# Seven small edits to a mixer kernel at once: load order and row work at the beginning, two ops moved between engines, p0 of even rows at the tails, slab differences spread over the first unit, one VectorE op ahead of the deferred work

## Chip, cores, metric

The kernel runs on one core of one Trainium2 chip. The metric is device time in microseconds (us), the median of several executions. Before the change it is 502.78 us (502.75 to 502.86, four executions). The granted clock of TensorE is recorded with each execution.

## The reference

With `xn` the layer norm of `x` (2048 rows of 576, bf16), the kernel computes a spectral mixer and a gated MLP of the same rows and combines them:

```python
xn = layernorm(x)
s  = irfft2(rfft2(xn) * (w_r + 1j * w_i))            # "A"
z  = gelu(xn @ w_in)                                  # 576 -> 4608
z1, z2 = z[..., :2304], layernorm(z[..., 2304:])
g  = (w_sp @ z2) + b_sp[:, None]                      # 2048 x 2048, over the rows
out = x + s * silu((z1 * g) @ w_out)
```

## The kernel before

TensorE (PE) runs one long list of matmuls.

**The beginning.** Loads are issued from two queues, SyncE (SP) and ScalarE (ACT). Rows are normalized on VectorE (DVE) in blocks of 128, `m` = 0..15; POOL (GpSimd) computes `(var + eps) ** -0.5`.

```python
nc.scalar.dma_start(out=ident[:], in_=cd_id.ap())
for m0, m1 in ((0, 1), (1, 2), (2, 4)):                       # x rows 0, 1, 2-3
    nc.sync.dma_start(out=XC[0][:, m0:m1, :], in_=xv[:, m0:m1, :])
for n in range(2):                                            # first two column groups of w_in, two loads each
    load_win_main(WIN2[...], slice(...), nc.scalar)
for g in range(3):
    (load_win if g else load_win_tail)(WIN2[...], slice(...)) # first the tails of the same groups
    if g == 0:
        nc.sync.dma_start(out=CDSD, in_=cd_cdsd.ap()...)      # the DFT matrix that p0 needs
    load_x(g + 1)
```

A DMA completion semaphore is used again eight loads later, so the cdsd load cannot be issued before x rows 2-3 have landed.

**The row pairs.** PE alternates between "chunks" of the MLP (`fill`: four full matmuls of 384 columns and a half-height "tail") and the first DFT of the rows (`p0`). p0 needs the transposed row (PE transpose, evicted from PSUM by ScalarE) and its fold, sum and difference of two halves, on VectorE:

```python
for m in range(2, MT):
    if m % 2 == 0:
        xpose(m + 1)
    p0_fold(m)                       # DVE, two tensor_tensor
    if m + 3 < MT:
        ln1(m + 3)                   # DVE: two bn_stats, one bn_aggr; POOL: var + eps, pow
    if m + 2 < MT:
        ln1_apply(m + 2)             # DVE: (x - mean) * rstd
    if m % 2 == 0:
        fill(1, 0)
        p0(m, True)
        fill(1, 0, lambda: p0_pair(m))   # tails of four chunks, then of p0(m) and p0(m+1)
    else:
        p0(m, False); p0_out(m)
        fill(1, 0)
        if m + 1 < MT:
            xpose(m + 1)
        fill(1, 0)
```

Chunks and transposes share four PSUM buffers, given out in the order in which they come free.

**The units.** The product over rows (`w_sp @ z2`) runs as 27 units, nine for each of three column blocks (units 0, 9, 18 begin a block; the third block has 256 columns instead of 384). Each unit has seven products P1, P6, P5, P7, P2, P4, P3 of eight matmuls, on sums and differences of the inputs. `tsum` makes such differences of the z2 blocks (which=2 on POOL), `slab_sums` those of `w_sp`. The order on VectorE is the program's order:

```python
def tsum(u, which):                       # cut
    if which == 0:   nc.vector.tensor_tensor(out=t, in0=zblk(p, 1, 1), in1=zblk(p, 0, 1), op=ALU.subtract)
    elif which == 1: nc.vector.tensor_tensor(out=t, in0=t2, in1=zblk(p, 0, 0), op=ALU.subtract)
    else:            nc.gpsimd.tensor_tensor(out=t, in0=zblk(p, 1, 0), in1=t2, op=ALU.subtract)

def main(u):                              # cut
    prod(a, "P1", zblk(p, 0, 0))          # PE
    nc.scalar.activation(out=p1, in_=a, func=ACT.Identity)
    nc.gpsimd.tensor_tensor(out=p1b, in0=p1, in1=B[1], op=ALU.add)
    prod(b, "P6", tb[u, 0])
    add(p1a, b, p1)                       # DVE, reads PSUM
    nc.gpsimd.tensor_tensor(out=ux, in0=p1a, in1=B[0], op=ALU.add)
    while later:                          # deferred DVE work of the stage before
        later.pop()()
    tsum(u + 1, 0)                        # DVE
    prod(c, "P5", zblk(p, 0, 1))
    prod(b, "P7", tb[u, 1], True)
    add(p1, b, p1b)                       # DVE; b is then free for P4
    u_sum(1, 1, c, p1)
    prod(a, "P2", zblk(p, 1, 0), True)
    tsum(u + 1, 2)                        # POOL
    u_sum(0, 0, a, B[0])                  # DVE
    prod(b, "P4", tb[u, 2], True)
    ...
    prod(c, "P3", zblk(p, 1, 1), True)    # reads the slabs that slab_sums(i, 0, 2) makes
```

Before unit 0: `tsum(0, 0)`, `tsum(0, 2)`, `tsum(0, 1)`, `slab_sums(0, 0, 2)`, `slab_sums(1, 0, 2)`; `slab_sums(2, 0, 2)` is in `later`.

## Time and profile before

| what | before |
|---|---|
| time, median | 502.78 us |
| span of the profiled execution | 501.5 us |
| PE busy | 492.1 us, 98% |
| row pair (start of p0 to start of p0 two rows on) | 5.20 us |
| PE waits from 206 to 216 us | 0.77 + 0.50 us |

From the page of the kernel before: the span, PE's busy time, and the granted TensorE clock in 40 slices (9 is 90% or more).

```profile
span 501.5 us, 9327 instructions
...
PE 492.1 (98%) x3454; PEld 310.4 (62%) x3454; DVE 329.8 (66%) x714; ACT 171.0 (34%) x355; POOL 210.8 (42%) x281
...
PEclk9999999999999999999999999999999999999999
...
PE 89%; ACT 4%; DVE 3%; DMA 2%; issue 1%; SPq 0%; DVEq 0%; ACTq 0%
```

PE is the limit: only time in which PE waits can be won. Where I give such waits, they are the gap between the starts of two matmuls, less the columns of the first at 2.4 per ns, the rate of this trace's back-to-back matmuls (384 columns every 0.162 us). A half-height matmul is counted with half its columns, since these start in pairs (at 10.58 and 10.58, 10.70 and 10.71 us in the trace of e11). The profiler's own idle times, in brackets in the lines below, are somewhat shorter, since it models the ends of matmuls.

From the timeline of the beginning (columns: start in us, duration, engine, line, operation, output and input, shape, count; in brackets the idle time of the engine just before and what ended it):

```profile
7.01 0.35 SPq L243 DMA_DIRECT2D AR<-c_cdsd  x1
7.02 0.82 DVE L258 BATCH_NORM_STATS2 st_165<-AR 128x6 f32<-128x288 bf16 x2 [0.66 <-DMA AR<-in_A_x_dram]
...
8.40 1.07 POOL L251 TENSOR_TENSOR rs<-ve,mhalf 128x1 f32<-128x1 f32 x2
...
8.99 0.41 DVE L281 TENSOR_SCALAR AR<-AR,mv_151,rs 128x512 bf16<-128x512 bf16 x1 [0.91 <-POOL rs L251]
...
10.32 0.66 PE L317 MATMUL pa<-AR 128*128 128x290 bf16 x4 [0.41 <-DMA AR<-c_cdsd]
...
12.05 0.32 PE L441 MATMUL ph<-AR 64*128 64x384 bf16 x1 [0.36 <-ACT AR L293]
```

x rows 2-3 land at 7.0 us; only then is cdsd issued, and the first p0 (L317) waits for it until 10.32. Row 1's pow (the first of the two at 8.40) stands behind row 2's variance op, and a chunk (L441) waits at 12.05 for a PSUM buffer, that is for ScalarE's eviction of a transpose (L293).

From the timeline of PE alone, one row pair:

```profile
19.56 0.81 PE L441 MATMUL ph<-AR 128*128 128x384 bf16 x4
20.47 0.67 PE L317 MATMUL pa<-AR 128*128 128x290 bf16 x4
20.98 1.24 PE L441 MATMUL ph<-AR 128*128 128x384 bf16 x8
...
22.40 0.67 PE L317 MATMUL pa<-AR 128*128 128x290 bf16 x4
...
25.66 0.67 PE L317 MATMUL pa<-AR 128*128 128x290 bf16 x4
```

Four matmuls of 384 columns take 0.65 us, but the p0 after the chunk at 19.56 starts 0.91 us after it: 0.26 us of waiting, in each of six row pairs (20.47 to 25.66: 5.19 us).

From the timeline around unit 0, and around the start of unit 18:

```profile
206.73 2.62 POOL L588 TENSOR_TENSOR AR<-Z_74,AR 128x1024 bf16<-128x1024 bf16 x1 [2.47 <-DVE AR L584]
207.28 3.21 DVE L523 TENSOR_TENSOR AR<-AR 128x1024 bf16<-128x1024 bf16 x2
...
211.02 1.46 PE L600 MATMUL pm<-AR 128*128 128x384 bf16 x8 [0.60 <-DVE AR L604]
...
427.17 0.81 DVE L667 TENSOR_TENSOR AR<-AR 128x576 bf16<-128x576 bf16 x1
...
427.90 0.68 DVE L584 TENSOR_TENSOR AR<-Z_74 128x1024 bf16<-128x1024 bf16 x1
...
428.87 2.13 POOL L588 TENSOR_TENSOR AR<-Z_74,AR 128x1024 bf16<-128x1024 bf16 x1
```

The slab differences (L523) take 0.68 us each elsewhere; two of them take 3.21 us beside POOL's subtraction (L588), and a product then waits.

### The profile page before, as it was taken

What the parts mean: (1) busy time and instruction counts of PE and PEld (TensorE: products, weight loads), DVE (VectorE), ACT (ScalarE), POOL (GpSimd) and SP (SyncE); (2) the same over time, 40 slices, a digit from 0 to 9 for tenths busy, and PEclk for the clock granted to TensorE, in tenths of its full rate; (3) what the DMA queues carried; (4) which work ended last, traced back from release to release, by engine and by line L of the source; (5) the groups of instructions that cost most, each with busy time, mean ns of one, the idle gap of its engine ahead of it and who ended that gap; (6) DMA issues with size and microseconds to landing.
All of it is one profiled execution on the core that took longest, in us unless ns stands there. A gap on an engine that the chain in (4) does not pass through costs nothing.

```text
span 501.5 us, 9327 instructions
## 1 busy us (share of the span) xinstructions
PE 492.1 (98%) x3454; PEld 310.4 (62%) x3454; DVE 329.8 (66%) x714; ACT 171.0 (34%) x355; POOL 210.8 (42%) x281
## 2 busy tenths in 40 slices
PE   7999999999999999999999999999999999999996
PEld 2655454555546544456666677666666678888885
DVE  5776588798646473966666547865656637877734
ACT  4878777686868755300000011000000011000001
POOL 2664323434242774554544501445355301666600
PEclk9999999999999999999999999999999999999999
DMA  7961688988373997581112499121121853111202
GB/s 233 322 198 49 241 272 258 320 240 222 121 257 118 212 252 208 182 274 58 38 33 64 110 167 216 39 63 33 35 61 33 171 137 93 48 48 46 80 26 71
DMA packets 86766, 70.82 MB, mean 141 GB/s; under 512 B 39776, under 2 KB 79328, under 8 KB 86464
## 3 DMA queue, kind: packets, MB, share of 16 engines
q1 hardware_dynamic: 80480, 55.69, 41.7%
q0 software_dynamic: 5008, 13.71, 8.2%
q10 hardware_dynamic: 1232, 0.82, 0.5%
q8 instruction: 27, 0.44, 0.4%
q14 instruction: 19, 0.16, 0.1%
HBM read 40.55 MB, written 21.26 MB: 123 GB/s over the span
## 4 chain that ended last, share of the span: by engine, by line
PE 89%; ACT 4%; DVE 3%; DMA 2%; issue 1%; SPq 0%; DVEq 0%; ACTq 0%
PE pm L600 42%; PE po L654 13%; PE ph L537 13%; PE ph L441 12%; ACT AR L322 2%; PE pa L415 2%; PE pb L374 2%; PE pa L317 2%; DMA AR<-in_A_x_dram 1%; PE pa L389 1%; ACT Z_74 L460 1%; DVE AR L523 1%; PE pa L362 1%; ACT AR L293 1%; DMA AR<-c_cdsd 1%
## 5 line engine op out<-in xcount | busy, mean ns | idle before, releaser
L600 PE MATMUL pm<-AR,Z_74 128*128 128x384 bf16 (+1 forms) x864 | 138.7, 308 | 0.0
L604 DVE TENSOR_TENSOR AR<-pm,AR 128x384 f32<-128x384 f32 (+3 forms) x162 | 82.4, 513 | 69.7 <-PE pm L600 66.5
L600 PEld LDWEIGHTS <-Z_74 128*128 128x128 bf16 x864 | 84.5, 98 | 40.6
L600 PE MATMUL pm<-AR 128*128 128x384 bf16 (+1 forms) x648 | 107.0, 308 | 1.0 <-DVE AR L604 0.9
L441 PE MATMUL ph<-AR 128*128 128x384 bf16 (+1 forms) x480 | 89.7, 327 | 1.4 <-ACT AR L293 0.9
L537 PE MATMUL ph<-AR 128*128 128x512 bf16 (+1 forms) x360 | 85.3, 379 | 0.0
L600 PEld LDWEIGHTS <-AR 128*128 128x128 bf16 x648 | 63.4, 98 | 31.9 <-issue 1.7
L614 ACT ACTIVATE AR<-pm 128x384 f32<-128x384 f32 (+1 forms) x27 | 12.3, 454 | 186.7 <-PE pm L600 186.7
L654 PE MATMUL po<-AR 128*128 128x288 bf16 x540 | 66.6, 286 | 0.0
L654 PEld LDWEIGHTS <-AR 128*128 128x128 bf16 x594 | 56.9, 98 | 13.9
L588 POOL TENSOR_TENSOR AR<-Z_74,AR 128x1024 bf16<-128x1024 bf16 x27 | 57.9, 2144 | 13.9 <-PE pm L600 10.6
L441 PEld LDWEIGHTS <-AR 128*128 128x128 bf16 (+1 forms) x480 | 40.1, 97 | 36.2 <-issue 13.2
L557 POOL DMA_DIRECT2D Z1d<-AR x55 | 31.9, 580 | 57.4 <-ACT AR L546 56.6
L615 POOL TENSOR_TENSOR AR<-AR 128x384 f32<-128x384 f32 (+1 forms) x27 | 22.8, 844 | 76.6 <-ACT AR L614 75.1
L537 PEld LDWEIGHTS <-AR 128*128 128x128 bf16 (+1 forms) x360 | 30.5, 97 | 29.3 <-issue 6.3
L546 ACT ACTIVATE AR<-ph 128x512 bf16<-128x512 f32 x72 | 42.1, 594 | 17.7 <-PE ph L537 16.8
L460 ACT ACTIVATE Z_74<-ph 128x384 bf16<-128x384 f32 x66 | 32.0, 502 | 23.8 <-PE ph L441 23.5
L657 ACT ACTIVATE TH<-po 128x576 f32<-128x576 f32 x15 | 9.8, 650 | 77.8 <-PE po L654 77.8
L618 POOL TENSOR_TENSOR AR<-AR 128x384 f32<-128x384 f32 (+1 forms) x27 | 30.4, 1128 | 11.9 <-DVE AR L604 11.9
L611 DVE TENSOR_TENSOR AR<-AR 128x384 bf16<-128x384 bf16 (+1 forms) x108 | 31.7, 335 | 0.9
L663 DVE SCALAR_TENSOR_TENSOR AR<-TH,po 128x576 bf16<-128x576 f32 x15 | 11.3, 754 | 30.0 <-ACT TH L657 29.9
L669 POOL DMA_DIRECT2D out_dram<-AR x12 | 6.6, 548 | 52.5 <-DVE AR L667 46.0
(183 smaller groups left out, 494.5 us busy)
## 6 DMA issues: line engine op xcount, KB each, us to landing
Z1d<-AR POOLq DMA_DIRECT2D x55, 128.0 KB, 3.9
AR<-Z1d SPq DMA_DIRECT2D x36, 192.0 KB, 3.1
AR<-in_A_x_dram SPq DMA_DIRECT2D x18, 144.0 KB, 3.1
AR<-in_B_w_out_dram SPq DMA_DIRECT2D x1, 2592.0 KB, 10.0
Ad<-AR POOLq DMA_DIRECT2D x16, 144.5 KB, 3.8
AR<-Ad SPq DMA_DIRECT2D x4, 578.0 KB, 6.0
AR<-in_A_w_r_dram SPq DMA_DIRECT2D x16, 144.5 KB, 4.2
AR<-in_A_w_i_dram SPq DMA_DIRECT2D x16, 144.5 KB, 3.9
```

The costliest lines, as they stand in the source:

```text
L441: nc.tensor.matmul(self.ph[:], lhsT=xnT[rows, self.m, ks, :], rhs=WIN2[rows, ks, n * ZC:(n + 1) * ZC], start=start, stop=stop)
L460: nc.scalar.activation(out=zc, in_=ph[:], func=ACT.Gelu_apprx_tanh)
L537: nc.tensor.matmul(self.ph[:].rearrange("p (a t) -> p a t", a=4), lhsT=wb[rows, ks, (fi % WG) * P:(fi % WG + 1) * P], rhs=xnT[rows, 4 * tq ...
L546: nc.scalar.activation(out=zs, in_=ph[:], func=ACT.Gelu_apprx_tanh)
L557: (nc.sync if place[0] > len(kinds) - 16 else nc.gpsimd).dma_start(out=d, in_=s_)
L588: nc.gpsimd.tensor_tensor(out=t, in0=zblk(p, 1, 0), in1=t2, op=ALU.subtract)
L600: nc.tensor.matmul(dst, lhsT=z[:, s, :], rhs=SLB[SA[name]][:, s, 0:nt], start=(s == 0 and not more), stop=(s == HM - 1), skip_group_check= ...
L604: nc.vector.tensor_tensor(out=out, in0=x, in1=y, op=ALU.add)
L611: nc.vector.tensor_tensor(out=o, in0=o, in1=zb[:, f, h, 0:nt], op=ALU.mult)
L615: nc.gpsimd.tensor_tensor(out=p1b, in0=p1, in1=B[1], op=ALU.add)
L618: nc.gpsimd.tensor_tensor(out=ux, in0=p1a, in1=B[0], op=ALU.add)
L654: nc.tensor.matmul(pv[:, hh, :], lhsT=U[:, fi, h, i * P:(i + 1) * P], rhs=WOUT[:, fi, c0 + hh * H2:c0 + hh * H2 + w // nh], start=(fi == 0 ...
```

## The change

The intent: fewer PE waits at the beginning, in the row pairs and before unit 0. The core of the diff, by part:

```diff
# A: second w_in group on the sync queue, behind the x rows
-  load_win_main(WIN2[...], slice(...), nc.scalar)
+  load_win_main(WIN2[...], slice(...), nc.sync if n else nc.scalar)
# B: var + eps of the first rows on VectorE
-  nc.gpsimd.tensor_scalar(out=ve[:], in0=mv[:, :, 1], scalar1=1e-5, ...)
+  eng.tensor_scalar(out=ve[:], in0=mv[:, :, 1], scalar1=1e-5, ...)
-            rs = rstd_of(mv, 1, "l11")
+            rs = rstd_of(mv, 1, "l11", nc.vector if m < 4 else nc.gpsimd)
# C: transpose 2 behind the fill
-  fill(1, 0, lambda: p0_pair(0), lambda: (xpose(1), p0(0, True), xpose(2)))
+  fill(1, 0, lambda: p0_pair(0), lambda: (xpose(1), p0(0, True)))
   ...
   fill(1, 0)
+  xpose(2)
   fill(1, 0)
# D: p0 of even rows at the tails
   fill(1, 0)
-  p0(m, True)
-  fill(1, 0, lambda: p0_pair(m))
+  fill(1, 0, lambda: p0_pair(m), lambda: p0(m, True))
# E: the first POOL subtraction on VectorE
-  nc.gpsimd.tensor_tensor(out=t, in0=zblk(p, 1, 0), in1=t2, op=ALU.subtract)
+  (nc.gpsimd if u else nc.vector).tensor_tensor(out=t, in0=zblk(p, 1, 0), in1=t2, op=ALU.subtract)
# F: one slab difference before unit 0, one in later, one (later2) behind u_sum(0, 0) of unit 0
-  later.append(partial(slab_sums, 2, 0, 2))
+  later.append(partial(slab_sums, 1, 0, 2))
+  later2.append(partial(slab_sums, 2, 0, 2))
-  for i in range(2):
-      slab_sums(i, 0, 2)
+  slab_sums(0, 0, 2)
# G: tsum of the next unit ahead of the deferred work, in every unit
   nc.gpsimd.tensor_tensor(out=ux, in0=p1a, in1=B[0], op=ALU.add)
+  tsum(u + 1, 0)
   while later:
       later.pop()()
-  tsum(u + 1, 0)
```

More of the change, by code (lines that the diff above doesn't have):

```diff
@@ L238 @@
     for n in range(2):
-        load_win_main(WIN2[:, :, n * ZC:(n + 1) * ZC], slice(Fh + n * ZC, Fh + (n + 1) * ZC), nc.scalar)
+        load_win_main(WIN2[:, :, n * ZC:(n + 1) * ZC], slice(Fh + n * ZC, Fh + (n + 1) * ZC), nc.sync if n else nc.scalar)
     for g in range(3):
@@ L245, with rstd_of @@
     nc.sync.dma_start(out=G1, in_=cd_g1.ap().rearrange("p (s k) -> p s k", s=N2))
-    def rstd_of(mv, n, tag):
+    def rstd_of(mv, n, tag, eng=nc.gpsimd):
         ve = small.tile([P, n], F32, tag=tag + "v")
-        nc.gpsimd.tensor_scalar(out=ve[:], in0=mv[:, :, 1], scalar1=1e-5, scalar2=one[:, 0:1], op0=ALU.add, op1=ALU.mult)
+        eng.tensor_scalar(out=ve[:], in0=mv[:, :, 1], scalar1=1e-5, scalar2=one[:, 0:1], op0=ALU.add, op1=ALU.mult)
         rs = small.tile([P, n], F32, tag=tag + "r", bufs=5)
@@ L628, in main @@
         u_sum(0, 0, a, B[0])
+        while later2:
+            later2.pop()()
         prod(b, "P4", tb[u, 2], True)
@@ L641, in load_xy @@
         nc.sync.dma_start(out=XIN[b], in_=xv[:, m, :])
-    later = []
+    later, later2 = [], []
     def outm(m, h, i, b, last, defer):
```

## The prediction

> **What bounds it now.** TensorE. The page shows PE busy 98% of a 501.5 us span, PEclk 9 throughout; the chain that ended last is 89% PE. Only idle PE time can be won. From the starts of successive matmuls (gap minus columns at 2.4 per ns, this trace's back-to-back rate) it is 3.0 us in 0-7, 2.7 us in 7-13, 0.26 us in each of six row pairs of 20-47 us, 0.77 + 0.50 us in 206-216 us.
>
> **1. Beginning.** The timeline shows x rows 2-3 landing at 7.0 although issued at 1.65: four w_in loads on the ScalarE queue share the bandwidth. The Trainium skill (DMA: Bandwidth & Descriptors, "Issuing engines are not separate DMA queues") says all queues run on the same 16 engines and interleave; this trace agrees: both move bytes until 7 us. The cdsd load issues only when those rows land (7.01) and lands at 10.3; the first p0 waits for it. With half of w_in behind x I estimate rows 2-3 at about 5.4 us (1.0 MB at some 290 GB/s), cdsd at about 9. ScalarE loses two issues, so its first Sqrt starts at about 4.2 instead of 4.58. The variance op on VectorE removes POOL's order (two 0.26 us adds before the first 0.55 us pow: row 1's rstd waited until 8.95 for row 2). Transpose 2 moves behind the fill, so no chunk waits for its PSUM buffer (0.61 us). Then VectorE's row work is the limit: second p0 near 10.5 us instead of 12.55; with the ScalarE evictions that follow I count **-1.8 us**.
>
> **2. Even rows.** In each row pair p0(m) starts 0.26 us late, waiting for VectorE's fold ("<-DVE AR L299"; period 5.20 us). A full chunk now goes first and covers it. The chunk's PSUM buffer comes free with the transpose's eviction (25.28 us), 0.1 us before it is wanted (25.41); ScalarE is busy 4.2 of 5.2 us: no new limit. Period 4.94 us, six times: **-1.6 us**.
>
> **3. Before unit 0.** POOL's 2.62 us subtraction (206.73-209.35) held VectorE's slab difference (2.61 us instead of 0.68), which delayed two adds: 1.27 us of PE idle. On VectorE it costs 0.68 us, and one slab instead of two precedes unit 0: both waits go. But the third slab difference now comes after product P2, at about 213.6, when POOL works at the next unit's subtraction (about 213.0-215.2). The Trainium skill (SBUF - State Buffer, "Who interferes with whom") says a VectorE instruction with two SBUF inputs and a GpSimd instruction that reads SBUF exclude each other for the whole instruction; the 2.61 us above agrees. Then the last product P3, wanted at 214.15, starts near 215.8: +1.6. Net **+0.4 us**; one chance in four of -1.2, POOL coming later than VectorE.
>
> **Sum.** -1.8 - 1.6 + 0.4: 502.8 to about 499.4 us, range 497.6 to 501.2. Faster by over 2% 0.01, within 0.98, slower 0.01.
>
> **What would show it.** x rows 2-3 land by 5.6, cdsd by 9.3, second p0 by 10.8 us; row-pair period 4.94, no PE wait for L299; no PE idle in unit 0's first six products, then 1-1.7 us before the seventh, with a VectorE slab difference of about 2.2 us beside POOL's subtraction.
>
> **What would make it wrong.** Another DMA order at the start; ScalarE's queue reordered, so the 0.26 us returns as a chunk's wait for PSUM; the bias load landing at another time, which decides who gets the port first; a later stage giving gains back.

## The result

The changed kernel takes 504.88 us (504.29 to 505.63, 4 executions) where the one before takes 502.78. The ratio is 1.0042, 95% interval 1.0025 to 1.0060: slower, not faster, and outside the predicted range. A ratio here and below is the mean time of one kernel's fast executions over that of the other's in the same rounds, so it is not quite the ratio of the medians that I quote.

The starts of the same matmuls in the two traces, in us, say where it went. The profiled execution of the changed kernel is the slowest of its four (505.63 us), so its parts add to a little more than the 2.1 us between the medians:

| point | before | after | difference | change over the stretch | predicted for it |
|---|---|---|---|---|---|
| p0 of row 3 | 17.20 | 17.83 | +0.63 | +0.63 | -1.8 |
| p0 of row 15 | 48.42 | 48.11 | -0.31 | -0.94 | -1.6 |
| first product of unit 0 | 206.35 | 206.05 | -0.30 | 0.0 | 0 |
| output of the first block | 289.51 | 289.92 | +0.41 | +0.71 | +0.4 |
| first product of unit 18 | 424.33 | 424.74 | +0.41 | 0.0 | 0 |
| output of the third block | 479.62 | 481.96 | +2.34 | +1.93 | 0 |
| end | 501.47 | 503.82 | +2.35 | 0.0 | 0 |

The same parts of the profile after. The page:

```profile
span 503.8 us, 9324 instructions
...
PE 491.8 (98%) x3454; PEld 311.5 (62%) x3454; DVE 330.5 (66%) x718; ACT 171.1 (34%) x355; POOL 207.9 (41%) x277
```

The shares are the same; a page of averages does not show this loss. The beginning, from the timeline:

```profile
6.37 0.56 POOL L251 TENSOR_TENSOR rs<-ve,mhalf 128x1 f32<-128x1 f32 x1 [4.57 <-DVE ve L249]
...
7.84 0.35 SPq L243 DMA_DIRECT2D AR<-c_cdsd  x1
7.85 0.82 DVE L258 BATCH_NORM_STATS2 st_165<-AR 128x6 f32<-128x288 bf16 x2 [1.56 <-DMA AR<-in_A_x_dram]
...
11.04 0.66 PE L317 MATMUL pa<-AR 128*128 128x290 bf16 x4 [1.05 <-DMA AR<-c_cdsd]
...
15.25 1.47 PE L441 MATMUL ph<-AR 128*128 128x384 bf16 x8 [0.42 <-ACT AR L293]
```

Row 1's pow does run early now (6.37), but x rows 2-3 land later than before (7.84), cdsd follows, and the first p0 waits 1.05 us for it. The wait for a PSUM buffer is not gone: it stands at 15.25.

The row pairs, PE alone:

```profile
21.50 0.66 PE L317 MATMUL pa<-AR 128*128 128x290 bf16 x4
...
23.00 0.67 PE L317 MATMUL pa<-AR 128*128 128x290 bf16 x4 [0.17 <-DVE AR L299]
...
26.66 0.66 PE L317 MATMUL pa<-AR 128*128 128x290 bf16 x4
...
31.60 0.66 PE L317 MATMUL pa<-AR 128*128 128x290 bf16 x4
```

Even rows (21.50, 26.66, 31.60) no longer wait. But every second odd row (23.00) waits for its own fold (L299): pairs of 5.16 and 4.94 us in turn.

Unit 0, and the start of unit 18:

```profile
213.11 2.11 POOL L588 TENSOR_TENSOR AR<-Z_74,AR 128x1024 bf16<-128x1024 bf16 x1
...
213.84 1.94 DVE L523 TENSOR_TENSOR AR<-AR 128x1024 bf16<-128x1024 bf16 x1
...
215.83 2.44 PE L600 MATMUL pm<-AR,Z_74 128*128 128x384 bf16 x14 [1.45 <-DVE AR L523]
...
427.10 0.68 DVE L584 TENSOR_TENSOR AR<-Z_74 128x1024 bf16<-128x1024 bf16 x1
...
428.48 2.13 POOL L588 TENSOR_TENSOR AR<-Z_74,AR 128x1024 bf16<-128x1024 bf16 x1 [0.17 <-PE pm L600]
428.66 2.26 DVE L669 TENSOR_TENSOR AR<-AR 128x576 bf16<-128x576 bf16 x1
...
431.31 1.03 PE L600 MATMUL pm<-AR 128*128 128x256 bf16 x8 [2.04 <-DVE AR L604]
```

In unit 0 the third slab difference (L523) starts while POOL subtracts and ends 0.55 us after POOL: the predicted wait before P3. At unit 18 the same thing happens where nothing was predicted: with tsum (L584) ahead of the deferred work, POOL's subtraction starts 0.18 us before the last deferred step (L669), which takes 2.26 us (the same kind of step took 0.46 us at 422.1 us before the change), and the adds behind it hold P4 for 2.2 us. Unit 9, where the order is the same and the products are longer, shows no such wait in the same trace: there the last deferred step takes 0.46 us and is done at 321.99 us, and POOL's subtraction starts at 322.87.

### The profile page after: what moved, and what is told of

Read it like the earlier page. It is cut to its first block, busy times and chain, and to the rows that moved or that the text cites. A ratio compares the mean times of both kernels' runs of the same rounds, so it can differ in the third digit from the quotient of the medians.

```text
span 503.8 us, 9324 instructions
## 1 busy us (share of the span) xinstructions
PE 491.8 (98%) x3454; PEld 311.5 (62%) x3454; DVE 330.5 (66%) x718; ACT 171.1 (34%) x355; POOL 207.9 (41%) x277
## 4 chain that ended last, share of the span: by engine, by line
PE 89%; DVE 3%; issue 2%; ACT 2%; DMA 2%; POOL 0%; SPq 0%; DVEq 0%; POOLq 0%; ACTq 0%
PE pm L600 41%; PE ph L537 13%; PE po L656 13%; PE ph L441 13%; PE pa L415 2%; PE pb L374 2%; PE pa L317 1%; DMA AR<-in_A_x_dram 1%; PE pa L389 1%; PE pa L362 1%; ACT AR L322 1%; PE pa L338 1%; ACT Z_74 L460 1%; DMA AR<-c_cdsd 1%; PE pt L292 0%
## 5 line engine op out<-in xcount | busy, mean ns | idle before, releaser
L588 POOL TENSOR_TENSOR AR<-Z_74,AR 128x1024 bf16<-128x1024 bf16 x26 | 55.3, 2128 | 11.8 <-PE pm L600 11.8
## 6 DMA issues: line engine op xcount, KB each, us to landing
AR<-in_B_w_out_dram SPq DMA_DIRECT2D x1, 2592.0 KB, 10.5
```

The lines of the kernel that those rows point to most:

```text
L588: (nc.gpsimd if u else nc.vector).tensor_tensor(out=t, in0=zblk(p, 1, 0), in1=t2, op=ALU.subtract)
```

## The experiments

Twelve kernels, in three groups of four; each was timed over five rounds against the kernel before on the same chip. On these chips the kernel before itself spreads over 1 to 2 us (502.12 to 504.19 in the first group), more than on the chip of the result.

### e1_tail_only: parts E, F, G alone

```diff
# against the kernel before
-  nc.gpsimd.tensor_tensor(out=t, in0=zblk(p, 1, 0), in1=t2, op=ALU.subtract)
+  (nc.gpsimd if u else nc.vector).tensor_tensor(out=t, in0=zblk(p, 1, 0), in1=t2, op=ALU.subtract)
-  later.append(partial(slab_sums, 2, 0, 2))
+  later.append(partial(slab_sums, 1, 0, 2))
+  later2.append(partial(slab_sums, 2, 0, 2))
-  for i in range(2):
-      slab_sums(i, 0, 2)
+  slab_sums(0, 0, 2)
   nc.gpsimd.tensor_tensor(out=ux, in0=p1a, in1=B[0], op=ALU.add)
+  tsum(u + 1, 0)
   while later:
       later.pop()()
-  tsum(u + 1, 0)
```

> Only the three edits of unit 0 and of the deferred work (first subtraction on VectorE, slab differences spread, tsum ahead of the deferred work). Theory 'port': these edits alone make the kernel slower, since the POOL subtraction of the next unit now starts before VectorE's two-SBUF-input work, which then waits for it: unit 0 +0.7 us and the start of the last column block +1.9 us, so +2.6 us, about 505.4 us. Rival 'start': the loss of the changed kernel comes from its beginning and its spread of 1.3 us; then this kernel is within 0.5 us of the one before or faster.

506.17 us (six executions), before 503.16; ratio 1.0060 (1.0043 to 1.0078). These three edits alone make the kernel slower by as much as the whole change does (1.0042; the intervals overlap), so the rival falls as the main cause. In the trace PE waits 1.31 us before P3 of unit 0 and 2.20 us from 428.9 us. The loss is larger than the waits, and the times fall into two groups: 505.41, 505.50, 505.54 and 506.80, 507.04, 507.26. The mean granted clock is 0.999 to 1.000 in the first group and 0.995 to 0.997 in the second. The profiled execution is of the second group. The busy time per stretch of that execution (columns: stretch in us, its length, busy time of PE, PEld, DVE, ACT, POOL with counts, granted clock, DMA share, GB/s):

```profile
424.00:428.00 4.00, 4.00 (x38) 3.52 (x37) 3.57 (x7) 1.03 (x2) 2.11 (x3) 1.00 0.11 37
428.00:431.40 3.40, 1.37 (x13) 1.07 (x12) 3.33 (x4) 0.00 (x0) 2.60 (x3) 1.00 0.00 0
431.40:434.80 3.40, 3.40 (x18) 2.33 (x17) 1.78 (x7) 0.00 (x0) 0.18 (x1) 0.51 0.11 43
434.80:438.20 3.40, 3.40 (x32) 3.04 (x31) 2.02 (x5) 0.38 (x1) 1.64 (x2) 0.99 0.26 77
```

After a stretch of 3.4 us in which PE was busy for 1.37 us, the granted clock is half for the next 3.41 us (431.44 to 434.85 in the clock record), and PE gets through 18 matmuls where the stretch after has 32. The Trainium skill (TensorE: Matmul & The Clock Gate, "What's actually happening") describes a free-running window of 3413 ns and a half-rate clock after an idle window. The trace agrees on the length: from the rise at 4.77 us to the fall at 431.44 are 426.67 us, 125 windows of 3.413 us. The stretches of full clock in the other traces are whole numbers of such windows too (498.35 us, 146 of them, in the two of the result). So in this kernel the same PE waits cost about 1.6 us more (the means of the two groups are 505.48 and 507.03) where a window takes in the whole wait; for the executions without a profile this is argued from their mean clock. The profiled execution of the changed kernel had the same 2.2 us wait without a fall: its clock rose at 6.69 us, and an estimate from there with windows of 3.413 us puts a window's end at 429.9, inside the wait (429.1 to 431.3).

### e2_sub_on_vector: part E alone

```diff
# against the kernel before
-  nc.gpsimd.tensor_tensor(out=t, in0=zblk(p, 1, 0), in1=t2, op=ALU.subtract)
+  (nc.gpsimd if u else nc.vector).tensor_tensor(out=t, in0=zblk(p, 1, 0), in1=t2, op=ALU.subtract)
```

> Only the first subtraction of unit 0 on VectorE; old order, two slab differences before unit 0, the third in the deferred work ahead of tsum. Theory 'port': without POOL busy, the slab differences take 0.68 us each and both PE waits before unit 0 (0.77 and 0.50 us) go: -1.2 us, about 501.5 us, and nothing changes at 424 us. Rival: VectorE's extra 0.68 us delays its adds as much as the POOL lock did; then 502.8 within 0.3.

502.18 us, ratio 0.9978 (0.9963 to 0.9993); in the trace unit 0 to the first output takes 81.90 us instead of 83.16, so 1.26 us are won (0.8 to 1.3 us against the 82.66 to 83.16 us of all seven traces with the old code there), and no PE wait over 0.15 us is left between 205 and 427 us. From the timeline of this kernel:

```profile
208.41 1.28 DVE L523 TENSOR_TENSOR AR<-AR 128x1024 bf16<-128x1024 bf16 x2
...
210.78 1.46 PE L600 MATMUL pm<-AR 128*128 128x384 bf16 x8
```

Two slab differences take 1.28 us instead of 3.21 when POOL is idle. Part E was right; F and G, added to it, took its gain away.

### e3_old_order: the whole change without G

```diff
# against the changed kernel
-  tsum(u + 1, 0)
   while later:
       later.pop()()
+  tsum(u + 1, 0)
```

> The whole change but with the deferred work ahead of tsum again. Theory 'port': the 2.2 us PE wait at the start of the last column block is gone (0.3 us left), about -1.9 us against the changed kernel, so 503.0 us; in unit 0 the wait before the seventh product stays, 1 to 1.7 us. Rival: the order matters little, because POOL's subtraction waits for a PE product in either order; then about 504.9 us.

502.69 us, ratio 0.9990 (0.9975 to 1.0005). The wait at unit 18 is 0.27 us, as before the change, because the last deferred step (L669) is done before POOL starts:

```profile
426.20 0.81 DVE L669 TENSOR_TENSOR AR<-AR 128x576 bf16<-128x576 bf16 x1
...
427.90 2.14 POOL L588 TENSOR_TENSOR AR<-Z,AR 128x1024 bf16<-128x1024 bf16 x1
```

In unit 0 the wait before P3 is 1.16 us. From the first product of unit 0 to the first output it takes 83.06 us; e2, which has E without F, takes 81.90. So spreading the slab differences (F) costs about 1.2 us, and the order (G) the 1.9 us of unit 18.

### e5_next_sub_on_vector: the whole change, the two colliding POOL subtractions on VectorE

```diff
-  (nc.gpsimd if u else nc.vector).tensor_tensor(out=t, in0=zblk(p, 1, 0), in1=t2, ...)
+  (nc.vector if u in (0, 1, 2 * NP + 1) else nc.gpsimd).tensor_tensor(out=t, in0=zblk(p, 1, 0), in1=t2, ...)
```

> The whole change, and the POOL subtraction of the next unit also on VectorE in the two places where VectorE had waited (units 0 and 18). Theory 'port': both waits (1.6 us before the seventh product of unit 0, 2.2 us at 429 us) go, although VectorE has 1.4 us more work; 3.5 us less than the changed kernel, about 501.4 us where before is 502.8, and the spread of more than 1 us of the changed kernel shrinks, because no idle stretch of 2 us is left in which the PE clock may be halved. Rival 'order of VectorE': VectorE is late there because of its own queue; then moving work onto it makes the waits longer.

502.20 us, ratio 0.9992 (0.9979 to 1.0005). The waits fall from 1.62 to 0.67 us and from 2.2 to 0.40 us although VectorE does more work: it was POOL's subtraction that held VectorE, not VectorE's own load. Of the 3.5 us expected about 2.5 came, by the two ratios (1.0042 less 0.9992, of 503 us; measured on two chips); the 0.67 us left are VectorE's own queue, which had waited 0.97 us for POOL's add of the bias. The spread did not shrink: 501.90 to 503.95. The profiled execution was the slowest, and its clock fell too, at the beginning:

```profile
6.00:9.40 3.40, 1.66 (x9) 0.51 (x8) 1.21 (x4) 0.71 (x2) 0.55 (x1) 1.00 0.62 176
9.40:12.80 3.40, 3.16 (x15) 1.51 (x16) 3.29 (x14) 0.70 (x1) 0.97 (x2) 0.50 1.00 324
```

Here PE waited 1.55 us for w_in and x rows 2-3, which landed at 8.63 and 8.35 us. My expectation that the spread comes from the 2 us waits alone was wrong: the beginning has the same weakness.

### e4_loads_only: part A alone

```diff
# against the kernel before
-  load_win_main(WIN2[...], slice(...), nc.scalar)
+  load_win_main(WIN2[...], slice(...), nc.sync if n else nc.scalar)
```

> Only the second half of the first w_in loads moved to the sync queue. Theory 'queue': the move itself makes x rows 2-3 (and the lane that the cdsd load waits for) later by about 0.8 us, first p0 at 11.0 instead of 10.3 us, about +0.7 us or 503.5 us. Rival 'phase': the later landing was chance of that one execution (DMA engines out of step, PE clock rising at 6.7 instead of 4.5 us); then rows 2-3 land by 7.0 us or earlier and the time is within 0.3 us of before, or better.

503.47 us, ratio 1.0002 (0.9987 to 1.0017); rows 2-3 landed at 7.09, cdsd at 10.44 us. So the move neither helps nor clearly harms, and the 7.82 us of the changed kernel were partly chance. But over all profiled executions the landings lean to later with A: 7.82, 7.13, 7.09, 8.35 us with A (mean 7.60); 6.99, 7.21, 7.46, 6.71, 6.69, 7.28, 6.50, 6.74 without (mean 6.95; e8 and e10, which order these loads otherwise, are left out). A landing is counted by 16 updates of its semaphore, and the last few trail: in the changed kernel the ninth came at 5.79, the fifteenth at 7.02 and the last at 7.82 us; before the change at 5.72, 6.62 and 6.99. So most of the load came no earlier with A, and the difference is in the last updates. Why A should make these later I can't say.

### e8_weights_behind_x: all four loads on the sync queue

```diff
-  load_win_main(WIN2[...], slice(...), nc.scalar)
+  load_win_main(WIN2[...], slice(...))
```

> All four first w_in loads on the sync queue behind the four x rows. Theory 'sharing': without a second queue x rows 2-3 land by 5 us, since nothing is ahead of them or beside them; the cdsd load, which waits for the same landing, lands by 8.5 us. Theory 'straggler': a landing is that of the slowest of 16 DMA engines, and these are out of step by 1.5 us whatever stands beside; then rows 2-3 still land after 6.3 us. In both the first chunk waits for w_in until about 7.5 us and the time stays within 1 us of before.

504.43 us (502.54 to 506.23), ratio 1.0026 (1.0006 to 1.0046). Rows 2-3 land at 5.32 us: the theory of sharing holds, nearly to the figure. The packets of the four x rows in the traces, by the time at which a share of them is done:

```
                         50%    90%    100%   landed
before                   3.48   5.16   6.54   6.99
after                    3.49   5.48   6.91   7.82
e8_weights_behind_x      3.10   4.26   4.91   5.32
```

Beside a second queue, the last tenth of the packets takes 1.4 us in these two traces, and the landing waits for it. That tail varies: in e11, also with a second queue, it took 0.73 us, hardly more than the 0.65 us of e8. What e8 alone shows is the earlier 90%. But nothing was gained. The three slowest of the six executions (504.56, 505.14, 506.23) have a mean granted clock of 0.993 to 0.997 and the others 1.000, so a part of the loss is the clock, as in e1. And cdsd still landed at 10.08 us (I had expected 8.5), since the same bytes stand ahead of it, and the first p0 started at 10.12.

Why A did not do a part of what e8 does is read from the landings before the change. The ScalarE queue's loads land in order: the first group at 4.53 and 7.33, the second at 8.28 and 8.79 us. The second group, which A moves, landed after the rows (6.99) anyhow. The packets say more than the landings: when 90% of the rows' packets were done (5.16 us), about 420 w_in packets were, fewer than the 512 of the first group, and that group stays where it was. In the last tenth of the rows' packets about 465 w_in packets went through before the change and about 450 after it. So A neither took bytes from ahead of the rows nor held the second group back while the last of them were under way.

### e12_variance_on_vector: part B alone

```diff
# against the kernel before
-  nc.gpsimd.tensor_scalar(out=ve[:], in0=mv[:, :, 1], scalar1=1e-5, ...)
+  eng.tensor_scalar(out=ve[:], in0=mv[:, :, 1], scalar1=1e-5, ...)
-            rs = rstd_of(mv, 1, "l11")
+            rs = rstd_of(mv, 1, "l11", nc.vector if m < 4 else nc.gpsimd)
```

> Only the variance op of the first rows on VectorE. Theory 'cdsd': row 1 is normalized 0.5 us earlier (8.4 to 8.5 instead of 8.99 us) but the first p0 still waits for the cdsd load, so the time is within 0.2 us of before. Rival: the earlier row moves everything after it and 0.5 us is won.

503.00 us, ratio 0.9999 (0.9986 to 1.0012). PE's wait for cdsd grew from 0.57 to 0.82 us: the earlier row only waits longer. As expected.

### e11_transpose_moved: part C alone

```diff
# against the kernel before
-  fill(1, 0, lambda: p0_pair(0), lambda: (xpose(1), p0(0, True), xpose(2)))
+  fill(1, 0, lambda: p0_pair(0), lambda: (xpose(1), p0(0, True)))
   ...
   fill(1, 0)
+  xpose(2)
   fill(1, 0)
```

> Only transpose 2 behind the fill. Theory 'moved wait': the 0.61 us wait for a PSUM buffer at 11.4 us goes and one of 0.5 to 0.6 us before the first chunk of the next row pair comes (a chunk waits for ScalarE's eviction of transpose 2); third and fourth p0 groups no earlier than before, time within 0.3 us of before. Rival: it is a real gain of 0.6 us, given back in the changed kernel by the loads.

502.89 us, ratio 0.9998 (0.9986 to 1.0010). The PE timeline of this kernel:

```profile
11.27 0.67 PE L317 MATMUL pa<-AR 128*128 128x290 bf16 x4 [0.28 <-DVE AR L299]
...
13.86 0.82 PE L441 MATMUL ph<-AR 128*128 128x384 bf16 x4
```

The 0.61 us wait at 11.4 us is gone; 0.50 us come before p0 of row 1, which waits for its fold, and 0.24 us before the chunk at 13.86, which waits for an eviction; 0.16 us of the first are the pause that this place has in every pair. The sum is the same (0.34 + 0.24). The wait moved as expected, though onto two places and with less on the one that I named.

### e6_rows_only: part D alone

```diff
# against the kernel before
   fill(1, 0)
-  p0(m, True)
-  fill(1, 0, lambda: p0_pair(m))
+  fill(1, 0, lambda: p0_pair(m), lambda: p0(m, True))
```

> Only p0 of even rows behind the chunk. Theory 'fold': the 0.26 us wait of each even row goes, but every second odd row then waits 0.2 us more for its own fold, which stands behind stats and apply on VectorE; row pairs of 4.94 and 5.15 us in turn, -0.9 us in all. Rival 'eviction': ScalarE's evictions give the loss; then the waits name ScalarE and the pairs are 5.2 us.

502.13 us, ratio 0.9983 (0.9970 to 0.9996). Every second odd row waits 0.37 to 0.38 us before its p0 where it had 0.16 (the pause of that place in every pair, from half-height to full-height matmuls), and the trace names the fold. From p0 of row 3 to that of row 15 it takes 30.27 us instead of 31.22: 0.95 us won, as the theory of the fold said. The eviction rival falls.

### e7_rows_and_early_fold: part D, with the odd row's fold moved ahead on VectorE

```diff
-            p0_fold(m)
-            if m + 3 < MT:
-                ln1(m + 3)
+            if m % 2 == 0:
+                p0_fold(m)
+            if m + 3 < MT:
+                ln1_stats(m + 3)
+            if m % 2 == 0:
+                p0_fold(m + 1)
+            if m + 3 < MT:
+                ln1_aggr(m + 3)
```

> As e6_rows_only, with the fold of the odd row ahead of the aggregation and the apply on VectorE. Theory 'fold': all row pairs take 4.94 us and no p0 waits, -1.5 us in all, 0.6 us better than e6. Rival 'eviction': the same as e6, with the wait put down to ScalarE.

501.20 us, ratio 0.9964 (0.9952 to 0.9976). The PE timeline of this kernel:

```profile
20.49 0.66 PE L317 MATMUL pa<-AR 128*128 128x290 bf16 x4
...
21.76 0.67 PE L317 MATMUL pa<-AR 128*128 128x290 bf16 x4
...
25.43 0.66 PE L317 MATMUL pa<-AR 128*128 128x290 bf16 x4
...
26.70 0.67 PE L317 MATMUL pa<-AR 128*128 128x290 bf16 x4
...
30.36 0.66 PE L317 MATMUL pa<-AR 128*128 128x290 bf16 x4
```

All pairs take 4.93 to 4.94 us. Rows 3 to 15 take 29.60 us, 1.62 us less than before. So the gain that I predicted for D was there, but D alone could not reach it.

### e9_rows_fold_sub: D, the early fold and E

```diff
# against e7_rows_and_early_fold
-  nc.gpsimd.tensor_tensor(out=t, in0=zblk(p, 1, 0), in1=t2, op=ALU.subtract)
+  (nc.gpsimd if u else nc.vector).tensor_tensor(out=t, in0=zblk(p, 1, 0), in1=t2, op=ALU.subtract)
```

> Only what paid in e2 and e7: p0 of even rows behind the chunk, the odd row's fold early, the first subtraction of unit 0 on VectorE; loads, variance op, transpose 2, slab differences and order as before. If the gains are of different stages they add: -1.5 and -1.2, about 500.1 us where before is 502.8 (ratio 0.9946). Rival: a gain in one stage is given back in a later one; then no better than e7 (ratio 0.9964).

500.31 us (499.88 to 501.32), before 502.97; ratio 0.9948 (0.9937 to 0.9960). The gains add, as expected (0.9946). This version is faster than both kernels, the one before and the changed one, and computes the right result.

### e10_and_cdsd_early: e9, with B and the cdsd load ahead of the tails

```diff
+    nc.sync.dma_start(out=CDSD, in_=cd_cdsd.ap()...)
     for g in range(3):
         (load_win if g else load_win_tail)(...)
-        if g == 0:
-            nc.sync.dma_start(out=CDSD, in_=cd_cdsd.ap()...)
         load_x(g + 1)
```

> e9 with the variance op on VectorE and the cdsd load issued ahead of the w_in tails, so that it waits for no landing. If the cdsd load is what holds the beginning: cdsd lands near 9 instead of 10.3 us, first p0 near 9.5, 0.4 to 0.9 us better than e9. Rival: the second half of w_in or the tails come later by the same amount and PE waits for them instead; then equal to e9.

501.36 us, ratio 0.9972 (0.9956 to 0.9988): 1 us worse than e9. Its two slowest executions (502.28 and 503.15) have a mean granted clock of 0.996 and 0.997; without them its mean is 0.6 us above that of e9. cdsd did land at 9.21 us, but the second w_in group landed at 9.72 and 10.86 us instead of 8.17 and 8.90 in e9, and PE waited for that (line numbers are one lower in this kernel):

```profile
10.91 0.65 PE L440 MATMUL ph<-AR 128*128 128x384 bf16 x3 [0.81 <-DMA AR<-in_B_w_in_dram]
...
11.67 0.66 PE L316 MATMUL pa<-AR 128*128 128x290 bf16 x4
```

The rival holds, and more than that: all of these bytes are needed by about 10 us, so pulling one load ahead puts another behind.

## Why the prediction was wrong, point by point

- **"With half of w_in behind x I estimate rows 2-3 at about 5.4 us", cdsd at 9, second p0 near 10.5, -1.8 us.** This step failed. Rows 2-3 landed at 7.82 us in the changed kernel and at 7.09 with part A alone. I took the total of bytes over the mean rate, as if the moved loads had stood ahead of the rows; the packets before the change already said otherwise: until 90% of the rows were in (5.16 us) no more w_in packets had moved than the first group has, and A leaves that group in place. And a landing is that of the last packet, 1.4 us after 90% of them, in the tail that A did not shorten. Nor did B and C give anything (ratios 0.9999 and 0.9998): with cdsd late, B's earlier row waits, and C's wait for a PSUM buffer moves on. At p0 of row 3 the changed kernel was 0.63 us behind, e3 0.07 us, and e5, with the halved clock of its beginning, 1.72 us: with A, B and C the start was early in none of the three traces. The Trainium skill's sentence that loads of all queues run on the same DMA engines and interleave (DMA: Bandwidth & Descriptors, "Issuing engines are not separate DMA queues") agrees with e4; I cited it and then used it only for one side.
- **"no new limit. Period 4.94 us, six times: -1.6 us."** The wait named did go, but a new limit came: p0 of the odd row now follows the even one sooner (1.27 us in e7, 1.93 before), and its fold stands on VectorE behind stats, aggregation and apply. I checked ScalarE and PSUM and not VectorE's order. It measured -0.94 us; with the fold moved (e7) -1.62.
- **Before unit 0, "Net +0.4 us".** The mechanism was right: the two waits went, the third slab difference met POOL's subtraction (1.94 us, predicted about 2.2), and PE waited 1.62 us before P3 (predicted 1 to 1.7). "no PE idle in unit 0's first six products" was not right: 0.37 us before P4, because the bias load landed at 211.15 us. Net +0.71 in place of +0.4. In e1, with the same parts E, F and G, the bias load landed 4.43 us after the unit's first product instead of 5.10, and unit 0 to the first output took 83.20 us, only 0.04 more than before the change; so a good part of the 0.71 comes from the time at which the bias load landed, which the prediction names as a risk. The rule behind it, from the Trainium skill (SBUF - State Buffer, "Who interferes with whom"), holds in the collisions seen here: VectorE's instruction ended 0.55 us after POOL's in unit 0 (before, after and e3) and 0.31 us after it at unit 18.
- **The sum had no term for the new order of tsum and the deferred work.** This is the largest loss, +1.93 us where nothing was forecast; only the beginning missed its forecast by more, 2.4 us. The prediction lists "a later stage giving gains back" among the things that would make it wrong, but gives it no amount. The diff applies it to every unit, and I looked at unit 0 alone. In unit 18 the products are shorter (1.04 us, against 1.46 us for eight matmuls in unit 0), so the deferred work is not done before POOL starts; in unit 9, with products of 1.46 us, it is. e3 shows it by undoing the order, e5 by taking POOL away.
- **What stays open.** Why the changed kernel's four executions spread over 1.3 us where the kernel before spread over 0.1 on the same chip. The halved clock explains the two groups of e1 and the slowest execution of e5, where the record shows it; the profiled execution of the changed kernel shows none after 6.69 us, and the mean clocks of the other three (0.998 to 1.000) leave no room for one, as half a clock for 3.41 us takes 0.003 off the mean. Nor is it settled why rows 2-3 tend to land later with A.

## What to carry to other kernels

When a change moves a wait, look for the next thing that becomes late on each engine involved, in its program order: here the same gain was 0.95 us or 1.62 us depending on one line on VectorE. An edit inside a loop has to be followed through every kind of iteration; the costliest effect here was in one that the change was not aimed at. And do not put VectorE work on two SBUF inputs where POOL is about to start a long instruction: move one of the two to the other engine, or before it.

## What the Trainium skill lacked or had wrong

- TensorE: Matmul & The Clock Gate, "What's actually happening" and the table under "Why this matters for your kernels": it speaks of an idle window, and of gaps over about 3 us. Here the clock was halved for 3.41 us after windows in which PE was busy for 1.37 of 3.40 us (e1, one wait of 2.2 us) and for 1.66 of 3.40 us (e5). In e1 a wait of 2.2 us inside one window was enough; that cost about 1.6 us more (the two groups of e1). The runs give no limit for the busy share: at the end of four traces (before, after, e1, e8) a window with 1.50 to 1.60 us of busy PE was followed by the full clock, at the end of two others (e6, e12) one with 1.31 and 1.17 us by half of it.
- SBUF - State Buffer, "Who interferes with whom": agrees (a 0.68 us instruction took 1.94 and 2.61 us beside POOL). It does not say how long after POOL the held VectorE instruction ends: 0.55 us for the slab differences, 0.31 us for the last deferred step at unit 18.
- DMA: Bandwidth & Descriptors: no section that I used says how far the packets of one load trail apart when a second queue is busy. Here 90% of the x packets were done by 5.16 us and the last at 6.54; without a second queue 4.26 and 4.91 (e8, one trace; the tail beside a second queue was as short as 0.73 us in e11).
